# A linear-attention recurrence with a feed-forward layer: a fixed instruction order and a software pipeline

## The chip, the core and the metric

The kernel runs on one core of a Trainium2 chip. Five engines work side by side, each with a queue of instructions of its own: TensorE (PE; its loads of stationary weights are listed as PEld), VectorE (DVE), ScalarE (ACT), GpSimd (POOL) and SyncE (SP), which issues most DMAs. They wait for one another through semaphores. The metric is device time in microseconds (us), and lower is better.

## What is computed

For each of 4 x 8 = 32 heads there is a state matrix of 40 x 40 that is carried through 768 time steps. The result y is then laid out as 3072 tokens of 320 features and goes through a feed-forward layer with squared ReLU.

```
for t in range(768):                       # all 32 heads, head size D = 40
    y[t]  = r[t] @ state
    Sa    = state @ a[t]
    state = state * w[t] - outer(Sa, b[t]) + outer(v[t], k[t])
x   = y as 3072 x 320
out = (relu(x @ w_in) ** 2) @ w_out        # 320 -> 2048 -> 320
```

## The kernel before

Time is cut into 6 chunks of 128 steps (loop variable c). Heads stand in pairs, two of 40 in 128 partitions (the halves 0 to 63 and 64 to 127, index s). A batch has 8 heads, that is 4 pairs; a quad is 2 pairs (4 heads), so a chunk has 4 batches and 8 quads (q), and the kernel 24 batches and 48 quads.

Work falls into three kinds.

- Preparation of a batch (`prep`): six loads of 160 KB (W, K, V, R, A, B; one row per time step and head, 160 bytes each); the logarithm of W on ACT (lnW, line 129); its running sum by a float32 matmul with a triangle (cs, line 132); two exponentials (GI and Gp, lines 135 and 136); casts of R, V, A and products of K, B with GI on POOL (lines 137 to 141); twenty transposes on PE (line 146) into t1 (R and V), t2 (Gp and K) and t3 (A); copies of these to SBUF on ACT (RVT line 155, GT line 160, KT line 161), and AT on DVE (line 164).
- A quad: `stage1` forms two 128 x 128 products per head (ec, lines 185 and 189; contraction over half of the partitions), which DVE masks into EVC (lines 193 and 194). `stage2` takes the carried state: z = state times R (line 207), copied by ACT into UZ (line 209); mx from AT and UZ (line 214, half of the rows) and from EVC (line 219, all rows), masked by DVE into MX (line 224); then uy collects an identity times UZ (IDb, line 227), K times EVC (line 232) and B times MX (line 237), the last two with half of the columns each. DVE scales uy into the next state UZ (line 241) and the output YS (line 244), and ut (line 250) turns the state for the next chunk's z, copied into UBD by two ACT instructions (line 253).
- The feed-forward layer of a chunk: `gather` brings YS into token order with eight DMAs (X<-YS, line 275); `ffn_in` is called 16 times (j), each with three hp matmuls (line 283), a relu on ACT (hs, line 287) and a square on DVE or POOL in turn (Gt, line 289); `ffn_out` is called 4 times, each with 16 op matmuls (line 295), an ACT copy (line 298) and a store.

The main loop writes, per quad, stage1 of the next quad, stage2 of this one, two or three `ffn_in` (or `ffn_out`) of the chunk before, and after each odd quad a preparation of the next chunk. All four batches of chunk 0 are prepared ahead of the loop, the weights are loaded behind that on POOL's queue. The last chunk's feed-forward layer stands alone behind the loop. A scheduler then reorders each engine's instructions; in PSUM five banks are shared by everything of the recurrence and of the preparation (pool `ps`), three by hp and op (pool `pf`).

Of the kernel before, what the change touches and what calls it, by code (L numbers as in the profile page):

```python
# [15 lines left out]
def kernel(  # L16
# [49 lines left out]
    MU4 = gl.tile([128, 2, 2, 128], BF16, name="MU4")  # L66
# [19 lines left out]
    for key in ("R", "A", "G", "V", "K", "B"):  # L86
        for i in range(2):
            heads = NHH if key in "RAG" else NH
            t_ = gl.tile([128, heads, 64], BF16, name=f"{key}p{i}")
            nc.any.memset(t_[:, :, D:64], 0.0)  # L90
            pads[key, i] = t_
    UZs = [gl.tile([128, NP, VC], BF16, name=f"UZ{i}") for i in range(2)]
# [4 lines left out]
    LOADS = ("W", "K", "V", "R", "A", "B")

    def load(c):
        got = {}  # L100
        for bb in range(NB):
            for key in LOADS:
                t_ = natp.tile([128, NHH, D], FP32, name=f"N{key}", tag=f"N{key}", bufs=5)
                nc.sync.dma_start(
                    out=t_[:],
                    in_=nat_srcs[key][bb, :, c * L:(c + 1) * L, :].rearrange("h t e -> t h e"))
                got[key, bb] = t_
        return got

    class Chunk:  # L110
        pass

    def chunk_tiles(c):
        ch = Chunk()
        ch.c = c
        ch.RV, ch.KT, ch.AT, ch.GT = [], [], [], []
        ch.EVC = {}
        ch.YS = chp.tile([128, NP, L], BF16, name="YS", tag="YS")
        ch.p = {key: pads[key, c % 2] for key in "KBV"}
        return ch  # L120

    def prep(ch, bb, nat):

        h0 = bb * NHH
        hs = slice(h0, h0 + NHH)
        P = ch.p
        Rp, Ap, Gp = (pads[key, bb % 2] for key in "RAG")
        lnW = ffp.tile([128, NHH * D], FP32, name="lnW", tag="lnW", bufs=2)
        nc.scalar.activation(out=lnW[:], in_=nat["W", bb][:].rearrange("p h e -> p (h e)"),  # L129
                             func=ACTF.Ln)  # L130
        cs = ps.tile([128, NHH, D], FP32, name="cs", tag="ps")
        nc.tensor.matmul(out=cs[:].rearrange("p h e -> p (h e)"), lhsT=UTI[:], rhs=lnW[:],  # L132
                         start=True, stop=True)
# [233 lines left out]
```

## Time and profile before

| | us |
|---|---|
| median of 3 runs (lowest, highest) | 369.28 (368.61, 370.23) |
| the profiled execution | 370.21 |
| its span, first to last instruction | 368.5 |
| PE busy | 308.7 |
| ACT busy | 187.0 |
| DVE busy | 171.3 |
| POOL busy | 142.0 |

The mean granted clock of PE is 0.943 of full speed. A matmul's duration in the trace includes the time through the array, and successive matmuls overlap; what one costs is read from the start of the next. Times in the rows are counted from the start of the span.

### The profile page before, as it was taken

What the parts mean: (1) busy time and instruction counts of PE and PEld (TensorE: products, weight loads), DVE (VectorE), ACT (ScalarE), POOL (GpSimd) and SP (SyncE); (2) the same over time, 40 slices, a digit from 0 to 9 for tenths busy, and PEclk for the clock granted to TensorE, in tenths of its full rate; (3) what the DMA queues carried; (4) which work ended last, traced back from release to release, by engine and by line L of the source; (5) the groups of instructions that cost most, each with busy time, mean ns of one, the idle gap of its engine ahead of it and who ended that gap; (6) DMA issues with size and microseconds to landing.
All of it is one profiled execution on the core that took longest, in us unless ns stands there. A gap on an engine that the chain in (4) does not pass through costs nothing. (4 is left out here: it accounts for less than half of the span.)

```text
span 368.5 us, 7042 instructions
## 1 busy us (share of the span) xinstructions
PE 308.7 (84%) x2600; PEld 163.2 (44%) x2600; DVE 171.3 (46%) x461; ACT 187.0 (51%) x392; POOL 142.0 (39%) x253
## 2 busy tenths in 40 slices
PE   2512676778799999999998999998999999999896
PEld 1302443444344555444554344554445545445454
DVE  3000346443745641854543854545673446873140
ACT  4521442444177555767355686346776536441371
POOL 4523533333165533465233465123554203430170
PEclk9999956655899999999999999999999999999999
DMA  9999999993852973972562551131000111001202
GB/s 151 178 153 175 180 185 178 179 163 69 125 105 39 154 133 87 165 124 41 109 125 62 83 91 25 49 64 46 0 3 0 37 45 29 3 2 50 58 2 72
DMA packets 163859, 32.58 MB, mean 88 GB/s; under 512 B 158384, under 2 KB 163504, under 8 KB 163824
## 3 DMA queue, kind: packets, MB, share of 16 engines
q1 hardware_dynamic: 161376, 29.50, 45.0%
q0 software_dynamic: 2448, 2.62, 4.6%
q8 instruction: 20, 0.33, 0.4%
q14 instruction: 15, 0.12, 0.1%
HBM read 28.84 MB, written 3.93 MB: 89 GB/s over the span
## 5 line engine op out<-in xcount | busy, mean ns | idle before, releaser
L283 PE MATMUL hp<-X,WIN 120*128 120x512 bf16 (+1 forms) x288 | 80.3, 384 | 1.9 <-DMA X<-YS 0.9
L287 ACT ACTIVATE hs<-hp 128x512 bf16<-128x512 f32 x96 | 55.2, 600 | 39.3 <-PE hp L283 30.5
L289 POOL TENSOR_TENSOR Gt<-hs 128x512 bf16<-128x512 bf16 x48 | 50.2, 1048 | 64.3 <-ACT hs L287 55.8
L253 ACT ACTIVATE UBD<-ut 40x256 bf16<-40x256 f32 x80 | 30.2, 377 | 47.4 <-PE ut L250 46.6
L193 DVE TENSOR_TENSOR EVC<-ec,MU 128x256 bf16<-128x256 f32 x96 | 40.0, 416 | 30.4 <-PE ec L189 29.2
L164 DVE TENSOR_TENSOR AT<-t,GT 128x512 bf16<-128x512 bf16 x24 | 10.1, 423 | 91.3 <-ACT GT L160 72.9
L224 DVE TENSOR_TENSOR MX<-mx,MX 128x336 bf16<-128x336 f32 x96 | 43.9, 499 | 13.2 <-PE mx L219 13.0
L179 POOL COPY EVC<-Vp 128x160 bf16<-128x160 bf16 x48 | 15.7, 330 | 87.1 <-PE uy L232 80.2
L194 DVE TENSOR_TENSOR EVC<-ec,MU 128x256 bf16<-128x256 f32 x96 | 39.8, 414 | 0.0
L295 PEld LDWEIGHTS <-Gt 128*128 128x128 bf16 x384 | 32.2, 98 | 15.0
L237 PE MATMUL uy<-MX,Bp 128*64 128x168 bf16 x192 | 29.3, 264 | 8.7 <-DVE MX L224 8.2
L289 DVE TENSOR_TENSOR Gt<-hs 128x512 bf16<-128x512 bf16 x48 | 27.3, 570 | 19.9 <-ACT hs L287 19.5
L283 PEld LDWEIGHTS <-WIN 120*128 120x128 bf16 (+1 forms) x288 | 23.0, 98 | 23.5 <-issue 2.7
L132 PE MATMUL cs<-lnW,UTI 128*128 128x320 f32 x48 | 24.2, 593 | 8.9 <-ACT lnW L129 8.9
L155 ACT ACTIVATE RVT<-t 128x1024 bf16<-128x1024 bf16 x24 | 24.7, 1029 | 12.9 <-PE t L146 12.8
L237 PEld LDWEIGHTS <-Bp 128*64 128x64 bf16 x192 | 13.1, 112 | 36.3 <-issue 36.0
L219 PE MATMUL mx<-EVC 128*128 128x168 bf16 x192 | 24.9, 252 | 1.4 <-DVE EVC L194 0.9
L140 POOL TENSOR_TENSOR Kp<-NK,GI 128x320 bf16<-128x320 f32 x24 | 20.6, 859 | 11.5 <-ACT GI L135 11.5
L137 POOL CAST Rp<-NR 128x320 bf16<-128x320 f32 x24 | 10.8, 449 | 30.8 <-DMA NR<-in_r_dram 16.5
L244 DVE TENSOR_TENSOR YS<-uy,GT 128x256 bf16<-128x256 f32 x48 | 20.0, 417 | 5.2 <-PE uy L237 5.1
L146 PE MATMUL t<-IDb,Rp 128*128 128x128 bf16 x96 | 11.2, 250 | 13.2 <-POOL Rp L137 13.2
L141 POOL TENSOR_TENSOR Bp<-NB,GI 128x320 bf16<-128x320 f32 x24 | 20.6, 859 | 2.5 <-DMA NB<-in_b_dram 2.5
(110 smaller groups left out, 448.1 us busy)
## 6 DMA issues: line engine op xcount, KB each, us to landing
NW<-in_w_dram SPq DMA_DIRECT2D x24, 160.0 KB
NK<-in_k_dram SPq DMA_DIRECT2D x24, 160.0 KB
NV<-in_v_dram SPq DMA_DIRECT2D x24, 160.0 KB
NR<-in_r_dram SPq DMA_DIRECT2D x24, 160.0 KB
NA<-in_a_dram SPq DMA_DIRECT2D x24, 160.0 KB
NB<-in_b_dram SPq DMA_DIRECT2D x24, 160.0 KB
out_dram<-osb SPq DMA_DIRECT2D x24, 160.0 KB
X<-YS SPq DMA_DIRECT2D x48, 40.0 KB
```

The lines of the kernel that those rows point to most:

```text
L132: nc.tensor.matmul(out=cs[:].rearrange("p h e -> p (h e)"), lhsT=UTI[:], rhs=lnW[:], start=True, stop=True)
L155: nc.scalar.activation(out=RV[:], in_=t1[:], func=ACTF.Copy)
L193: nc.vector.tensor_tensor(out=dst[:, :, 0:L], in0=ec[s][:, 0], in1=MU4[:, 0], op=ALU.mult)
L194: nc.vector.tensor_tensor(out=dst[:, :, L + D:], in0=ec[s][:, 1], in1=MU4[:, 1], op=ALU.mult)
L219: nc.tensor.matmul(out=mx[s][:, i, :], lhsT=EVC[:, i, s, 0:L], rhs=EVC[:, i, s, L:], start=(c == 0), stop=True, skip_group_check=True)
L224: nc.vector.tensor_tensor(out=MX[:, s], in0=mx[s][:], in1=MX2[:], op=ALU.mult)
L237: nc.tensor.matmul(out=uy[half(s), i, :], lhsT=ch.p["B"][:, 4 * q + 2 * i + s, :], rhs=MX[:, s, i, :], start=False, stop=True, skip_group_ ...
L253: nc.scalar.activation(out=UBD[64 * s:64 * s + D, p2, :], in_=ut[64 * s:64 * s + D, :, :], func=ACTF.Copy)
L283: nc.tensor.matmul(out=hp[:], lhsT=WIN[g][0:rows[g], j * 128:(j + 1) * 128], rhs=ch.X[g][0:rows[g]].rearrange("p a b -> p (a b)"), start=( ...
L287: nc.scalar.activation(out=hs[:], in_=hp[:], func=ACTF.Relu)
L289: eng.tensor_tensor(out=ch.Gt[:, j].rearrange("p a b -> p (a b)"), in0=hs[:], in1=hs[:], op=ALU.mult)
L295: nc.tensor.matmul(out=op_[:], lhsT=ch.Gt[:, j, bb, :], rhs=WOUT[:, j, :], start=(j == 0), stop=(j == NJ - 1))
```

## The change

The order of each engine's instructions is taken as the code writes it (`manual_schedule`). The code is cut into parts, and a step per quad writes them: ec of the next quad, z and IDb, a filler, ut of the quad before, mx, a filler, parts of a preparation, K, B, a filler, further parts. A filler is one `ffn_in` or half an `ffn_out`; it starts three steps behind the end of its chunk. A table (`when`) says which step prepares which batch; chunk 0 starts after one batch. The loads are issued batch by batch, six ahead; the weights after step 5, the gather in two parts (after quads 5 and 7), the last one from three queues.

In PSUM ec, mx and uy get banks of their own with one buffer each (five banks), hp and op two, and t1, t2, t3, cs and ut share one (`pp`; in the first five batches the preparation uses those of hp). z is formed in uy's bank and stays there as a part of the sum, so that IDb carries only the state's columns. One mask instruction per half covers both products of ec; UZ is scaled in two halves; UBD is copied in one instruction. A square is issued one piece later than its relu. UZ is set to zero at the start by POOL.

```diff
-    ps = ctx.enter_context(tc.tile_pool(name="ps", bufs=5, space=PSUM))
-    pf = ctx.enter_context(tc.tile_pool(name="pf", bufs=3, space=PSUM))
+    ps = ctx.enter_context(tc.tile_pool(name="ps", bufs=1, space=PSUM))
+    ctx.enter_context(tc.manual_schedule())
...
+    def load(m):
+
+        c, bb = divmod(m, NB)
+        for key in ("W", "K", "B", "R", "V", "A"):
+            t_ = natp.tile([128, NHH, D], FP32, name=f"N{key}", tag=f"N{key}")
+            nc.sync.dma_start(
+                out=t_[:],
+                in_=nat_srcs[key][bb, :, c * L:(c + 1) * L, :].rearrange("h t e -> t h e"))
+            nat[key, m] = t_
+
+    AHEAD = 6
+    for m in range(AHEAD):
+        load(m)
...
+        t_ = gl.tile([128, NP, UWP], BF16, name=f"UZ{i}")
+        nc.gpsimd.memset(t_[:], 0.0)
...
+    def where_pp(m):
+        return {"tag": "ff", "bufs": 2} if m < 5 else {"tag": "pp"}
...
+        if m + AHEAD < NBC:
+            load(m + AHEAD)
...
+    def prep_rv(m):
+        o = bt[m]
+        o.RV = chp.tile([128, 2, PB, L], BF16, name="RVT", tag="RVT", bufs=4)
+        t1 = ps.tile([128, 2, PB, L], BF16, name="t1", **where_pp(m))
...
+        ec = [ps.tile([128, 2, 2, L], FP32, name=f"ec{s}", tag=f"ec{s}") for s in range(2)]
...
-            nc.vector.tensor_tensor(out=dst[:, :, 0:L], in0=ec[s][:, 0], in1=MU4[:, 0], op=ALU.mult)
-            nc.vector.tensor_tensor(out=dst[:, :, L + D:], in0=ec[s][:, 1], in1=MU4[:, 1],
-                                    op=ALU.mult)
...
+            nc.vector.tensor_tensor(out=spread(EVC[:, :, s, 0:L], L + XO[s]), in0=ec[s][:],
+                                    in1=MU4[:].rearrange("p (i u) x -> p i u x", u=2), op=ALU.mult)
+
+    def st_z(st):
+
+        c, o, j0, p2 = where(st)
+        UZ = UZs[c % 2]
+        uy = uys[st] = ps.tile([128, 2, UW], FP32, name="uy", tag="uy")
         if c > 0:
-            z = ps.tile([128, 2, L], FP32, name="z", tag="ps")
             for i in range(2):
-                nc.tensor.matmul(out=z[:, i, :], lhsT=UBD[:, 2 * q + i, :],
-                                 rhs=ch.RV[bb][:, 0, j0 + i, :], start=True, stop=True)
-            nc.scalar.activation(out=UZ[:, p2, D:VC], in_=z[:], func=ACTF.Copy)
-        mx = [ps.tile([128, 2, VC], FP32, name=f"mx{s}", tag="ps") for s in range(2)]
+                nc.tensor.matmul(out=uy[:, i, D:D + L], lhsT=UBD[:, p2.start + i, :],
+                                 rhs=o.RV[:, 0, j0 + i, :], start=(i == 0), stop=False,
+                                 skip_group_check=True)
+            nc.scalar.activation(out=UZ[:, p2, D:D + L], in_=uy[:, :, D:D + L], func=ACTF.Copy)
+        nc.tensor.matmul(out=spread(uy[:, :, 0:D], VC), lhsT=IDb[:],
+                         rhs=spread(UZ[:, p2, 0:D], VC), start=(c == 0), stop=False,
+                         skip_group_check=True)
...
+        mx = [ps.tile([128, 2, VC], FP32, name=f"mx{s}", tag=f"mx{s}") for s in range(2)]
...
-            nc.tensor.matmul(out=uy[:].rearrange("p a b -> p (a b)"), lhsT=IDb[:],
-                             rhs=UZ[:, p2, :].rearrange("p a b -> p (a b)"),
-                             start=True, stop=False, skip_group_check=True)
...
+        for s in range(2):
+            for i in range(2):
+                nc.tensor.matmul(out=uy[half(s), i, D * s:D * s + VC],
+                                 lhsT=o.B[:, 2 * (j0 + i) + s, :], rhs=MX[:, s, i, :],
+                                 start=False, stop=True, skip_group_check=True)
...
+            for u in range(2):
+                nc.vector.tensor_tensor(
+                    out=UZs[(c + 1) % 2][half(u), p2, VC * u:VC * u + D],
+                    in0=uy[half(u), :, VC * u:VC * u + D],
+                    in1=gl_[half(u)].to_broadcast([64, 2, D]), op=ALU.mult)
...
+        ut = ps.tile([128, 2, 128], FP32, name="ut", tag="pp")
...
+        nc.scalar.activation(out=UBD[:, p2, :], in_=ut[:], func=ACTF.Copy)
...
+        hp = ps.tile([128, NB * L], FP32, name="hp", tag="ff", bufs=2)
...
+        later.append(lambda: eng.tensor_tensor(out=Gt[:, j].rearrange("p a b -> p (a b)"),
+                                               in0=hs[:], in1=hs[:], op=ALU.mult))
...
+    def ffn_out(c, bb, part):
+        flush()
+        if part == 0:
+            ops[c, bb] = ps.tile([128, DM], FP32, name="op_", tag="ff", bufs=2)
+        op_ = ops[c, bb]
+        for j in range(part * NJ // 2, (part + 1) * NJ // 2):
...
+    def filler(st):
+        if fill and fill[0][0] <= st:
+            fill.pop(0)[1]()
...
+    when = {}
+    for m in range(1, NBC):
+        first = 2 * m - 2 if m < 5 else {5: 8, 6: 10, 7: 11}.get(m, 2 * m - 4)
+        last = first if 5 <= m < 8 else first + 1
+        for st, lot, f in ((first, 0, prep_cast), (first, 1, prep_decay), (first, 2, prep_rv),
+                           (last, 1, prep_gk), (last, 2, prep_a)):
+            when.setdefault((st, lot), []).append((f, m))
+    def prepare(st, lot):
+        for f, m in when.pop((st, lot), []):
+            f(m)
+    for f in (prep_cast, prep_decay, prep_rv, prep_gk, prep_a):
+        f(0)
+    st_ec(0)
+    for st in range(NS):
+        c, q = divmod(st, NQ)
+        late = c == 0 and q % 2 == 1
+        prepare(st, 0)
+        if not late and st + 1 < NS:
+            st_ec(st + 1)
+        st_z(st)
+        filler(st)
+        if st > 0:
+            st_u(st - 1)
+        st_mx(st)
+        filler(st)
+        prepare(st, 1)
+        st_k(st)
+        st_b(st)
+        filler(st)
+        prepare(st, 2)
+        if late:
+            st_ec(st + 1)
+        if st == 5:
+            load_weights()
+        if q == 5:
+            gather(c, 0, 3, [nc.sync])
+        if q == 7:
+            gather(c, 3, 4, [nc.sync] if c + 1 < NCH else [nc.sync, nc.scalar, nc.gpsimd])
+            fill += [(st + 3, lambda c=c, j=j: ffn_in(c, j)) for j in range(NJ)]
+            fill += [(st + 3, lambda c=c, b_=b_, p_=p_: ffn_out(c, b_, p_))
+                     for b_ in range(NB) for p_ in range(2)]
+    flush()
+    while fill:
+        fill.pop(0)[1]()
```

On PE, at the end of a quad of chunk 1 (K and B into uy, op of the feed-forward layer), there stood before:

```order
L295 LDWEIGHTS Gt_1054
L295 MATMUL op__1659<-WOUT_124,Gt_1054 128x320
L237 LDWEIGHTS Bp1_118
L237 MATMUL uy_1537<-MX_1534,Bp1_118 64x168
L295 LDWEIGHTS Gt_1054
L295 MATMUL op__1659<-WOUT_124,Gt_1054 128x320
L295 LDWEIGHTS Gt_1054
L295 MATMUL op__1659<-WOUT_124,Gt_1054 128x320
L237 LDWEIGHTS Bp1_118
L237 MATMUL uy_1537<-MX_1534,Bp1_118 64x168
L237 LDWEIGHTS Bp1_118
L237 MATMUL uy_1537<-MX_1534,Bp1_118 64x168
```

On PE, at the same place of a quad of chunk 1, there stands now:

```order
L260 MATMUL uy_1598<-EVC_1482,Kp3_191 64x168
L260 LDWEIGHTS Kp3_191
L260 MATMUL uy_1598<-EVC_1482,Kp3_191 64x168
L270 LDWEIGHTS Bp3_199
L270 MATMUL uy_1598<-MX_1626,Bp3_199 64x168
L270 LDWEIGHTS Bp3_199
L270 MATMUL uy_1598<-MX_1626,Bp3_199 64x168
L270 LDWEIGHTS Bp3_199
L270 MATMUL uy_1598<-MX_1626,Bp3_199 64x168
L270 LDWEIGHTS Bp3_199
L270 MATMUL uy_1598<-MX_1626,Bp3_199 64x168
L353 LDWEIGHTS Gt_1045
```

The four B matmuls (line 237, now 270) were split by op matmuls and stood apart from K; now they follow K without a break, and the feed-forward work comes behind them.

On SP, around the gather of chunk 0 (X), there stood before, behind 66 loads:

```order
L104 DMA NW_501<-in_w_dram 128x8x40
L104 DMA NK_503<-in_k_dram 128x8x40
L104 DMA NV_505<-in_v_dram 128x8x40
L104 DMA NR_507<-in_r_dram 128x8x40
L104 DMA NA_509<-in_a_dram 128x8x40
L104 DMA NB_511<-in_b_dram 128x8x40
L275 DMA X0_974<-YS_176 40x4x128 x3
L275 DMA X1_975<-YS_176 40x4x128 x3
L275 DMA X2_976<-YS_176 40x4x128 x2
```

On SP, at the gather of chunk 0, there stands now, behind 60 loads:

```order
L320 DMA X0_706<-YS_345 40x3x128 x3
L320 DMA X1_707<-YS_345 40x3x128 x3
L320 DMA X2_708<-YS_345 40x3x128 x2
L63 DMA NW_761<-in_w_dram 128x8x40
L63 DMA NK_763<-in_k_dram 128x8x40
L63 DMA NB_765<-in_b_dram 128x8x40
L63 DMA NR_767<-in_r_dram 128x8x40
L63 DMA NV_769<-in_v_dram 128x8x40
L63 DMA NA_771<-in_a_dram 128x8x40
L320 DMA X0_706<-YS_345 40x128 x3
L320 DMA X1_707<-YS_345 40x128 x3
L320 DMA X2_708<-YS_345 40x128 x2
```

The gather stood behind twelve batches of loads; its first part now stands behind ten, its second behind eleven.

## Rows read from the trace of the kernel before

**Rows 1.** Stretches: length, PE, PEld, DVE, ACT, POOL busy, clock, DMA, GB/s.

```profile
0.00:80.00 80.00, 42.45 (x308) 25.77 (x310) 23.87 (x71) 30.35 (x62) 30.68 (x74) 0.83 1.08 171
42.00:105.00 63.00, 46.35 (x387) 26.92 (x385) 31.27 (x89) 25.54 (x56) 21.19 (x48) 0.67 0.89 142
105.00:335.00 230.00, 218.22 (x1946) 110.06 (x1944) 128.05 (x344) 133.13 (x283) 94.77 (x154) 1.00 0.34 65
```

**Rows 2.** Timeline of PE, one quad: start, length, instructions, idle time and what ended it.

```profile
218.09 0.26 PE L237 MATMUL uy<-MX,Bp 128*64 128x168 bf16 x1
218.28 0.61 PE L283 MATMUL hp<-X,WIN 120*128 120x512 bf16 x2
218.82 0.33 PE L237 MATMUL uy<-MX,Bp 128*64 128x168 bf16 x3
219.08 0.82 PE L283 MATMUL hp<-X,WIN 120*128 120x512 bf16 x3
219.84 0.29 PE L250 MATMUL ut<-IDS,UZ 128*40 128x128 bf16 x4
220.06 0.29 PE L185 MATMUL ec<-AT,KT 64*128 64x128 bf16 x4
...
220.39 0.29 PE L207 MATMUL z<-RVT,UBD 128*128 128x128 bf16 x2
220.51 0.81 PE L283 MATMUL hp<-X,WIN 120*128 120x512 bf16 x3
221.65 0.32 PE L214 MATMUL mx<-UZ,AT 64*128 64x168 bf16 x4 [0.32 <-ACT UZ L209]
221.90 0.46 PE L219 MATMUL mx<-EVC 128*128 128x168 bf16 x4
222.20 0.31 PE L227 MATMUL uy<-UZ,IDb 128*128 128x336 bf16 x1
222.44 0.34 PE L232 MATMUL uy<-EVC,Kp 128*64 128x168 bf16 x4
222.71 0.82 PE L283 MATMUL hp<-X,WIN 120*128 120x512 bf16 x3
```

**Rows 3.** The chain that ended last, its end: start, length, what.

```profile
344.60 2.12 DMA X<-YS
...
347.25 0.61 ACT hs L287
...
347.90 8.63 PE hp L283 x39
...
363.05 2.19 PE op__5046 L295 x16
```

**Rows 4.** Timeline of PE, the preparation of a batch.

```profile
212.00 0.81 PE L132 MATMUL cs<-lnW,UTI 128*128 128x320 f32 x2
212.65 0.39 PE L146 MATMUL t<-IDb,Rp 128*128 128x128 bf16 x4
212.87 0.39 PE L146 MATMUL t<-IDb,Vp 128*128 128x128 bf16 x4
...
214.43 0.40 PE L146 MATMUL t<-IDb,Kp 128*128 128x128 bf16 x4 [0.30 <-POOL Kp L140]
```

**Rows 5.** Timeline of PE, two quads of chunk 0 apart, and the first hp.

```profile
60.00 0.36 PE L185 MATMUL ec<-AT,KT 64*128 64x128 bf16 x4
...
71.65 0.40 PE L185 MATMUL ec<-AT,KT 64*128 64x128 bf16 x4
...
99.95 1.34 PE L283 MATMUL hp<-X,WIN 120*128 120x512 bf16 x3
```

**Rows 6.** Groups by line: busy time, mean ns of one, idle time before.

```profile
L155 ACT ACTIVATE RVT<-t 128x1024 bf16<-128x1024 bf16 x24 | 24.7, 1029 | 12.9 <-PE t L146 12.8
```

**Rows 7.** Timeline of all engines, the first AT.

```profile
12.22 0.42 DVE L164 TENSOR_TENSOR AT<-t,GT 128x512 bf16<-128x512 bf16 x1 [7.66 <-ACT GT L160]
```

**Rows 8.** Timeline of SP, the issue of chunk 0's gather.

```profile
84.33 6.89 SPq L275 DMA_DIRECT2D X<-YS  x8
```

More of the change, by code (lines that the diff above doesn't have):

```diff
@@ L85 @@
-    pads = {}
[L86 to L92, printed above, removed]
-    UBD = gl.tile([128, NP, 128], BF16, name="UBD")
-    nc.any.memset(UBD[:], 0.0)
-    nat_srcs = {"W": w, "K": k, "V": v, "R": r, "A": a, "B": b}
@@ L97 @@
[L97 to L110, printed above, removed]
-        pass
[L113 to L120, printed above, removed]
@@ L143, in transposes @@
-        def transposes(dst, pad, h):
-            for j in range(PB):
-                src = pad[:, h + 2 * j:h + 2 * j + 2, :].rearrange("p a b -> p (a b)")
-                nc.tensor.transpose(out=dst[:, j, :], in_=src, identity=IDb[:])
-        RV = chp.tile([128, 2, PB, L], BF16, name="RVT", tag="RVT", bufs=8)
-        KT = chp.tile([128, PB, L], BF16, name="KT", tag="KT", bufs=8)
-        AT = chp.tile([128, PB, L], BF16, name="AT", tag="AT", bufs=8)
-        GT = chp.tile([128, PB, L + 2], BF16, name="GT", tag="GT", bufs=8)
@@ L230, in stage2 @@
         for i in range(2):
             for s in range(2):
[L232 to L234 removed]
+                nc.tensor.matmul(out=uy[half(s), i, D * s:D * s + VC],
+                                 lhsT=o.K[:, 2 * (j0 + i) + s, :], rhs=EVC[:, i, s, L:],
+                                 start=False, stop=False, skip_group_check=True)
@@ L257 @@
-    WIN = []
+                nc.tensor.matmul(out=ut[half(s), i, :],
+                                 lhsT=UZn[:, p2.start + i, VC * s:VC * s + 64],
+                                 rhs=IDb[:], start=True, stop=True)
+        nc.scalar.activation(out=UBD[:, p2, :], in_=ut[:], func=ACTF.Copy)
+    YSs, Xs, Gts, WIN = {}, {}, {}, []
     rows = [3 * D, 3 * D, 2 * D]
@@ L333 @@
-    for j in range(NJ):
-        ffn_in(prev, j)
-    for bb in range(NB):
-        ffn_out(prev, bb)
+        Gt = Gts[c]
+        later.append(lambda: eng.tensor_tensor(out=Gt[:, j].rearrange("p a b -> p (a b)"),
+                                               in0=hs[:], in1=hs[:], op=ALU.mult))
+    ops = {}
+    def ffn_out(c, bb, part):
[4 more added lines that the diff above has]
+        for j in range(part * NJ // 2, (part + 1) * NJ // 2):
+            nc.tensor.matmul(out=op_[:], lhsT=Gts[c][:, j, bb, :], rhs=WOUT[:, j, :],
+                             start=(j == 0), stop=(j == NJ - 1))
+        if part == 1:
+            osb = ffp.tile([128, DM], FP32, name="osb", tag="osb")
+            nc.scalar.activation(out=osb[:], in_=op_[:], func=ACTF.Copy)
+            tok = bb * T + c * L
+            nc.sync.dma_start(out=out[tok:tok + L, :], in_=osb[:])
```

275 lines of the change are left out of this document (132 added, 143 removed).

## The prediction

> **What bounds the kernel now.** I read three views in this order: busy time by stretch, the order of matmuls on TensorE (PE) within one quad, and the sync queue (SP). The stretches [rows 1] show two regimes. From 105 to 335 us PE is busy 218.2 of 230.0 us at the full granted clock: the end is set by how much PE must do and by what its hand-overs cost. From 42 to 105 us it is busy 46.4 of 63 us and the clock is granted at 0.67 on average, between its levels of 1.2 and 2.4 GHz: here PE waits in each quad for VectorE (DVE). The DMA engines move 171 GB/s over the first 80 us, nothing of which is spare: 13.7 MB. The weights' share of it is 2 x 2048 x 320 numbers of two bytes, 2.62 MB.
>
> Within a quad of the busy stretch [rows 2] the starts tell more than the durations, since matmuls are pipelined. Three hp take 0.22 us each, but from the third to a ut, which uses 40 of the array's columns, it takes 0.10 us more (219.08 to 219.84). The same 0.10 us stands at every change between full-array, half-row (ec, mx from AT) and half-column (K, B, ut) matmuls; z to hp, both full, shows none (0.12 us for two z). A quad of before changes eleven times.
>
> **The stretch with feed-forward work, steps 10 to 47 (a step is a quad).** By starts in [rows 2] one quad of before costs PE: B 0.19 and 0.26 (split around hp), ut 0.22, ec 0.33, z 0.12, mx 0.25 and 0.30, the IDb matmul 0.24, K 0.27, together 2.18, and four entries from hp at 0.10: 2.58 us. Afterwards B follows K with nothing between (K 0.27 - 0.10 = 0.17; B 0.07 + 0.26 = 0.33), and IDb moves 160 columns for 336 (0.14 less its change, halved: 0.07) and stands behind z without a change. That is 0.33 + 0.12 + 0.07 + 0.22 + 0.25 + 0.30 + 0.17 + 0.33 = 1.79, with three entries 2.09 us. The saving is 0.49 us per quad. All other terms stay: an hp 0.22 (8.63 us for 39), an op 0.136 (2.19 for 16) [rows 3], a preparation 0.65 for cs and five times 0.22 for its transposes, 1.75 us [rows 4].
>
> Steps 10 to 47 hold 38 quads, 18 preparations (batches 6 to 23) and 114 pieces: 80 of ffn_in (three hp, 0.66 us) and 34 halves of ffn_out (eight op, 1.09 us). PE's sum: 38 x 2.09 = 79.4, less 7 x 0.22 where the last chunk has no ut, = 77.9; 52.8; 37.0; 18 x 1.75 = 31.5. Together 199.2 us.
>
> Stalls come on top. Before, from the first hp at 99.95 [rows 5] to the last chunk's X at 346.7 [rows 3], 246.8 us pass. The same prices give 38 x 2.58 - 8 x 0.32 = 95.4 for quads, 5 x 19.3 = 96.4 for five chunks of feed-forward and 16 x 1.75 = 28.0 for the preparations that the code leaves for it: 219.8. So 27 us, 0.71 per quad, were waits: mx for ScalarE's (ACT) copy of z (0.32 at 221.65 [rows 2]), the transposes of Kp for GpSimd (POOL) (0.30 at 214.43 [rows 4]). Both places now have a filler and other parts between. But the order is fixed, so nothing else can step in, and ec, mx, uy have one buffer each, while cs, t1, t2, t3 and ut share one bank: each of the six uses in two steps waits until ACT has read the one before, behind ACT's relus. The longest such read is 1.03 us (RVT [rows 6]). The bound from below is 0, from above 1.1 us per step (that read once per step, fully exposed). I take 0.5, nearer to the 0.71 of before less the waits with cover: 34 steps with preparations, 17 us. Batches 6 and 7 go through all parts in one step; there Kp's transposes wait for Exp and multiply as before, and K and B of the quad stand behind: 1.5 us each (0 to 3), 3 us.
>
> DVE: one mask of 512 elements replaces two of 256, UZ's scaling becomes two instructions: less than a tenth of a microsecond either way per quad, hidden while DVE is below PE (128.1 of 230 us [rows 1]). The single UBD copy takes work from ACT; I cost both at nothing. If ACT or DVE were full, that is the first rival.
>
> **The start.** In before all four batches are prepared before the first quad, and weights move between the loads. Afterwards quad 0 needs batch 0 alone. Before's first AT is ready at 12.6 us [rows 7]. Two new memsets of 3712 elements on POOL stand ahead of its first casts and delay this; I put quad 0 at 13 to 20 us. Two quads with a preparation took 11.65 us at the low clock (60.00 to 71.65 [rows 5]); the new pairs have the same chain (masks, MX, YS). Five pairs bring step 10 to 72 to 79 us.
>
> Step 10 holds the first hp, and that needs X. Here **a new wait** comes. On SP the gather's second half stands behind batch 10's loads, and each DMA waits for the one eight places ahead to land. So X needs 11 batches x 0.983 MB = 10.81, the weights' 2.62 (POOL's queue, after step 5) and 0.25 for the first half: 13.68 MB. At 171 GB/s [rows 1] that is 80 us; the last gather's issue (6.89 us for eight [rows 8], so 0.86) and landing (2.12 us [rows 3]) make it 83, and I take 84 (80 to 88). PE's queue is in order, so mx, K and B of step 10 and all behind wait with the hp. Whether step 10 is reached at 65 or 80 us is then worth nothing; putting the weights later gains little, since their bytes are still ahead of X. The wait probably lowers the clock again: 2 us (0 to 4).
>
> **The tail.** Six pieces of chunk 4, all ffn_out halves, are left after step 47: 6 x 1.09 = 6.5 us, which cover the last gather (landing 2.12 us, three queues). Then sixteen ffn_in: the ff pool has two buffers instead of three, so a relu (0.61 us with its hand-over in [rows 3], about 0.7) sets the pace rather than 0.66: 11.5 us. Eight halves 8.7. Together 26.7 us. From the last matmul to the end of the span 368.5 - 365.2 = 3.3 us stay [rows 3].
>
> **The sum.** 84 + 2 + 199.2 + 17 + 3 + 26.7 + 3.3 = 335 us of span. The profiled execution took 370.21 us for a span of 368.5, and the median of the runs is 0.9 below it; so 335 + 1.7 - 0.9 = 336 us. Against before that is 16 us from the earlier first hp, some 25 from quads and waits behind it, and 8 back in the tail, of which 6.5 are work moved there.
>
> **The rivals.** First, ACT through the shared bank sets the pace: stalls of 1.1 us in each of 34 steps instead of 0.5, 20 us more, 356 us. For it speaks that six uses of one bank per two steps each take a read by ACT; against it that ACT was busy 133.1 of 230 us [rows 1] and that op steps leave it idle.
>
> Second, X comes early: the queue moves faster than in before, or the transfers of loads and weights overlap better, and PE reaches the first hp at its own pace near 68 us. That gives 320 us. Against it stand the 171 GB/s, at a DMA share above 1 [rows 1].
>
> Third, on the slow side: the clock. Where before had a wait of about a microsecond in each quad, 42 to 105 us, the granted clock was 0.67 [rows 1]; where PE was busy 95% it was 1.00. With one buffer for each of five banks, waits in every step could bring that state to steps 10 to 47. Some 165 of the 199 us are streaming, which takes twice as long at 1.2 GHz, so from about a fifth of the stretch at the low level (34 us) the change loses; at a third of it the time is 390 us. Against it: the sum above leaves PE about 90% busy.
> On this the Trainium skill, TensorE: Matmul & The Clock Gate, section "A second HAM failure mode: psum-queue depth-cycling", speaks against the change: cycling through PSUM banks makes PE idle briefly between groups often enough that its clock swings between the two levels. By that rule the third rival would be the likeliest and the time near its 390; the trace of before, with its own cycling of five banks at clock 1.00 from 105 to 335 us, does not bear it out.
>
> **How the numbers follow.** Forecast 0.60 (336 us, by its own bounds 318 to 348); first rival 0.18 (356); second 0.13 (320); third 0.05 (390); 0.04 for faster stretches than all of these (stalls near 0, below 318). The range of 310 to 358 leaves out the third rival and the ends of the others. The low end is X at 80, stalls of 3 us and no loss in relus: 80 + 199.2 + 3 + 25 + 3.3 + 0.8 = 311; the high end is the first rival with 2 us more for X. Faster by over 0.5% (about what a measurement of this kernel can tell from no change): 0.60 + 0.18 + 0.13 + 0.04 less 0.02 for stalls that eat it all, 0.93; the same 0.02; slower 0.05.
>
> **What would show it.** The first hp in the new trace at 80 to 88 us, with PE idle before it for 5 us or more and an X DMA as what ended it; no more than three entries per quad, B 0.17 us behind K; two steps with ffn_in pieces 10.5 to 11 us apart, with ffn_out 12.5 to 13; hp in the tail 0.7 us per piece. The prediction is wrong if the first hp starts by 75 us (then the second rival), if PE idles over 1 us per step on ACT behind cs, t or ut (the first), or if the granted clock is below 1.00 in the stretch after the first hp (the third).

## The result

The changed kernel takes 359.34 us (median of 4, 358.58 to 360.8) against 369.75 us before in the same comparison: ratio 0.973, 95% interval 0.968 to 0.977. It is faster, by 10 us and not by the 33 forecast; 336 us and the range up to 358 were both too low.

The same three stretches as in [rows 1], of the kernel after (length, PE, PEld, DVE, ACT, POOL busy, clock, DMA share, GB/s):

```profile
0.00:80.00 80.00, 46.80 (x409) 29.07 (x409) 44.85 (x109) 25.25 (x50) 34.05 (x71) 0.75 1.06 165
42.00:105.00 63.00, 35.14 (x249) 19.38 (x248) 20.45 (x46) 15.59 (x32) 13.90 (x32) 0.57 0.87 140
105.00:335.00 230.00, 202.22 (x2019) 120.04 (x2019) 125.35 (x293) 126.79 (x265) 104.21 (x193) 1.00 0.35 69
```

The clock is at its upper level from 105 us on, as before. But PE is busy for 202.2 of 230 us there instead of 218.2: some 12% of the stretch is idle. What PE waited for is in the next view, five rows of PE's waits over the whole span (waiting line, released by: us in total, times, longest):

```profile
PE uy L231 <- ACT UZ L230: 26.4, 40, 0.9
PE hp L335 <- DMA X<-YS: 16.3, 3, 13.8
PE ec L207 <- DVE AT L186: 5.9, 7, 1.1
PE t L162 <- ACT RVT L170: 3.3, 3, 1.1
PE t L162 <- ACT Gp L152: 2.7, 3, 0.9
```

The second row is the wait for X that was forecast. The first is in no term of the sum: L231 is the IDb matmul, and L230 is ACT's copy of z. Every one of the 40 quads that have a z pays it. In the timeline of PE over two steps (start, length, instructions, idle time and its end; to be held against [rows 2]) it looks like this:

```profile
165.50 0.28 PE L207 MATMUL ec<-AT,KT 64*128 64x128 bf16 x4
...
165.82 0.28 PE L227 MATMUL uy<-RVT,UBD 128*128 128x128 bf16 x2
167.05 0.23 PE L231 MATMUL uy<-UZ,IDb 128*128 128x160 bf16 x1 [0.94 <-ACT UZ L230]
167.12 0.81 PE L335 MATMUL hp<-X,WIN 120*128 120x512 bf16 x3
...
169.84 0.34 PE L260 MATMUL uy<-EVC,Kp 128*64 128x168 bf16 x4
170.01 0.31 PE L270 MATMUL uy<-MX,Bp 128*64 128x168 bf16 x4
170.26 0.82 PE L335 MATMUL hp<-X,WIN 120*128 120x512 bf16 x3
...
171.85 0.29 PE L227 MATMUL uy<-RVT,UBD 128*128 128x128 bf16 x2
172.61 0.23 PE L231 MATMUL uy<-UZ,IDb 128*128 128x160 bf16 x1 [0.47 <-ACT UZ L230]
...
177.15 0.28 PE L207 MATMUL ec<-AT,KT 64*128 64x128 bf16 x4
```

From z to IDb 1.23 us pass in one step and 0.76 in the next, where the sum had 0.12. The longer one is the step in which ACT reads RVT (1.02 us) ahead of z. Two steps take 11.65 us (165.50 to 177.15), not 10.5 to 11. The rest of the quad is as priced: B 0.17 us behind K, three entries from full-array matmuls.

IDb and the copy touch no common column: IDb writes columns 0 to 40 and 168 to 208 of each half of uy, ACT reads 40 to 168. The program holds a semaphore between them all the same. Two things are shared, the bank of uy and the tile UZ in SBUF, of which IDb reads columns 0 to 40 and 168 to 208 and the copy writes those between; which of the two makes the wait is tried below (z twice). On the bank the Trainium skill, PSUM — Partial Sum Buffer, section "PSUM bank collisions raise a hardware error", says that two engines have to be kept apart by bank (within each 32 partitions) and not by address, since disjoint columns collide too. The trace agrees as far as it can: the wait stands in all 40 quads. By that page it can't be left out, and no run here leaves it out; the order and the bank can be chosen.

PE's start of the feed-forward work and the steps behind it, to be held against the last row of [rows 5]:

```profile
70.76 0.29 PE L231 MATMUL uy<-UZ,IDb 128*128 128x160 bf16 x1 [0.47 <-ACT UZ L230]
84.82 0.58 PE L335 MATMUL hp<-X,WIN 120*128 120x512 bf16 x1 [13.78 <-DMA X<-YS]
87.07 0.59 PE L335 MATMUL hp<-X,WIN 120*128 120x512 bf16 x1 [1.66 <-DMA X<-YS]
88.55 0.59 PE L335 MATMUL hp<-X,WIN 80*128 80x512 bf16 x1 [0.89 <-DMA X<-YS]
...
99.97 0.29 PE L207 MATMUL ec<-AT,KT 64*128 64x128 bf16 x4 [0.58 <-DVE AT L186]
...
110.62 0.29 PE L207 MATMUL ec<-AT,KT 64*128 64x128 bf16 x4
```

The first hp starts at 84.82 us, forecast 84. X comes in three parts and is whole only at 88.55, and steps 10 and 11 then last until 110.62.

### The profile page after: what moved, and what is told of

Same layout as the page of the kernel before. It is cut to its first block, busy times and chain, and to the rows that moved or that the text cites. A ratio compares the mean times of both kernels' runs of the same rounds, so it can differ in the third digit from the quotient of the medians.

```text
span 356.9 us, 7113 instructions
## 1 busy us (share of the span) xinstructions
PE 281.4 (79%) x2608; PEld 165.9 (46%) x2608; DVE 178.3 (50%) x421; ACT 168.4 (47%) x345; POOL 151.4 (42%) x280
## 4 chain that ended last, share of the span: by engine, by line
PE 61%; ACT 16%; DVE 7%; issue 7%; SPq 5%; POOL 1%; DMA 1%; ACTq 0%; DVEq 0%; POOLq 0%
PE hp L335 15%; PE t L162 6%; PE mx L248 6%; ACT hs L339 4%; ACT UZ L230 4%; PE cs L148 4%; SPq L320 3%; PE uy L231 3%; PE uy L260 3%; PE mx L243 3%; DVE EVC L217 3%; ACT RVT L170 3%; PE ut L294 3%; PE uy L270 2%; SPq L63 2%
## 5 line engine op out<-in xcount | busy, mean ns | idle before, releaser
L335 PE MATMUL hp<-X,WIN 120*128 120x512 bf16 (+1 forms) x288 | 80.3, 391 | 16.9 <-DMA X<-YS 16.3
L217 DVE TENSOR_TENSOR EVC<-ec,MU 128x512 bf16<-128x512 f32 x96 | 61.7, 684 | 22.4 <-PE ec L211 17.4
L231 PE MATMUL uy<-UZ,IDb 128*128 128x160 bf16 x48 | 11.8, 246 | 26.8 <-ACT UZ L230 26.4
L170 ACT ACTIVATE RVT<-t 128x1024 bf16<-128x1024 bf16 x24 | 24.5, 1020 | 13.7 <-PE t L162 13.7
L342 DVE TENSOR_TENSOR Gt<-hs 128x512 bf16<-128x512 bf16 x48 | 20.9, 435 | 17.6 <-ACT hs L339 17.4
L207 PE MATMUL ec<-AT,KT 64*128 64x128 bf16 x192 | 15.5, 229 | 11.8 <-DVE AT L186 5.9
L215 POOL COPY EVC<-Vp 128x80 bf16<-128x80 bf16 x96 | 24.0, 279 | 0.0
L297 ACT ACTIVATE UBD<-ut 128x256 bf16<-128x256 f32 x40 | 15.2, 379 | 18.3 <-PE ut L294 18.3
L178 ACT ACTIVATE GT<-t 128x512 bf16<-128x512 bf16 x24 | 14.3, 598 | 18.8 <-PE t L162 18.7
L230 ACT ACTIVATE UZ<-uy 128x256 bf16<-128x256 f32 x40 | 15.4, 385 | 11.3 <-PE uy L227 10.6
L280 DVE TENSOR_TENSOR UZ<-uy,GT 64x80 bf16<-64x80 f32 x80 | 18.7, 234 | 0.5
L270 PE MATMUL uy<-MX,Bp 128*64 128x168 bf16 x192 | 17.6, 249 | 0.2
```

What stands on the lines that cost most here:

```text
L170: nc.scalar.activation(out=o.RV[:], in_=t1[:], func=ACTF.Copy)
L217: nc.vector.tensor_tensor(out=spread(EVC[:, :, s, 0:L], L + XO[s]), in0=ec[s][:], in1=MU4[:].rearrange("p (i u) x -> p i u x", u=2), op=AL ...
L230: nc.scalar.activation(out=UZ[:, p2, D:D + L], in_=uy[:, :, D:D + L], func=ACTF.Copy)
L270: nc.tensor.matmul(out=uy[half(s), i, D * s:D * s + VC], lhsT=o.B[:, 2 * (j0 + i) + s, :], rhs=MX[:, s, i, :], start=False, stop=True, ski ...
L335: nc.tensor.matmul(out=hp[:], lhsT=WIN[g][0:rows[g], j * 128:(j + 1) * 128], rhs=Xs[c][g][0:rows[g]].rearrange("p a b -> p (a b)"), start= ...
L342: later.append(lambda: eng.tensor_tensor(out=Gt[:, j].rearrange("p a b -> p (a b)"), in0=hs[:], in1=hs[:], op=ALU.mult))
```

## Experiments: the wait of the IDb matmul

**IDb ahead of z.** Theory W: the IDb matmul's wait for ACT in uy's bank is what is missing. Rival A is the first rival of the prediction: ACT and the shared bank set the pace.

```
+        nc.tensor.matmul(out=spread(uy[:, :, 0:D], VC), lhsT=IDb[:],
+                         rhs=spread(UZ[:, p2, 0:D], VC), start=True, stop=False,
...
         if c > 0:
...
-                                 rhs=o.RV[:, 0, j0 + i, :], start=(i == 0), stop=False,
+                                 rhs=o.RV[:, 0, j0 + i, :], start=False, stop=False,
...
             nc.scalar.activation(out=UZ[:, p2, D:D + L], in_=uy[:, :, D:D + L], func=ACTF.Copy)
-        nc.tensor.matmul(out=spread(uy[:, :, 0:D], VC), lhsT=IDb[:],
-                         rhs=spread(UZ[:, p2, 0:D], VC), start=(c == 0), stop=False,
...
```

> Edit: the IDb matmul is issued ahead of the two z matmuls instead of behind them; it now clears the uy bank, z adds to it. Nothing else moves. Theory W (the IDb matmul waits for ScalarE's copy of z in the same bank: 26.4 us in 40 quads of the changed kernel, 22.2 of them in 33 quads between 120 and 320 us): the wait goes, the filler follows z at once and covers the copy, two steps with ffn_in come down from 11.65 to 10.3 to 10.7 us, the time to 333 to 340 us. Rival A (ScalarE and the bank that cs, t1 to t3 and ut share set the pace): the same waits come back at ut, mx or the transposes, two steps stay at 11.3 us or more, the time at 354 to 359 us.

329.73 us (329.56 to 330.06), ratio to before 0.890 (0.885 to 0.894): 30 us less than the changed kernel, by one matmul that stands three rows higher. PE of this kernel, the start of one step and of the step two before it, then the stretch from 120 to 280 us, and below it the same stretch of the kernel after:

```profile
115.67 0.29 PE L207 MATMUL ec<-AT,KT 64*128 64x128 bf16 x4
...
125.61 0.28 PE L207 MATMUL ec<-AT,KT 64*128 64x128 bf16 x4
...
125.94 0.24 PE L225 MATMUL uy<-UZ,IDb 128*128 128x160 bf16 x1
126.02 0.28 PE L230 MATMUL uy<-RVT,UBD 128*128 128x128 bf16 x2
126.13 0.81 PE L335 MATMUL hp<-X,WIN 120*128 120x512 bf16 x3
```

```profile
120.00:280.00 160.00, 158.88 (x1679) 97.90 (x1678) 105.38 (x250) 103.87 (x222) 85.78 (x164) 1.00 0.43 83
```

```profile
120.00:280.00 160.00, 141.03 (x1453) 84.46 (x1452) 93.31 (x223) 92.59 (x196) 77.51 (x146) 1.00 0.41 79
```

PE has no idle time left (158.9 of 160 us). The wait doesn't come back elsewhere: of mx for the copy there are two waits of 0.4 us together. Two steps take 9.94 us (115.67 to 125.61), less than the 10.3 that was expected at least.

**IDb behind mx.** The same matmul, in the other direction: from behind z to behind the mx matmuls.

```
-        nc.tensor.matmul(out=spread(uy[:, :, 0:D], VC), lhsT=IDb[:],
...
+        nc.tensor.matmul(out=spread(uys[st][:, :, 0:D], VC), lhsT=IDb[:],
...
         MX = mxs[st] = qdp.tile([128, 2, 2, VC], BF16, name="MX", tag="MX")
```

> Edit: the IDb matmul is issued behind the mx matmuls from EVC, between the first filler and the second, instead of right behind z. Theory W: as with the IDb matmul ahead of z, 333 to 340 us, since filler and mx lie between the copy of z and its reader in the bank; it may be some us better, since z is not delayed by 0.07 us. Rival A: 354 to 359 us.

331.16 us (328.59 to 332.07), ratio 0.892 (0.887 to 0.897), not to be told from IDb ahead of z. Both places do it, so it is the place directly behind z that costs, not the matmul.

**z twice.** The order of the changed kernel stays, IDb right behind z; only the bank that ACT reads is another.

```
+            z = ps.tile([128, 2, L], FP32, name="z", tag="pp")
+            for i in range(2):
+                nc.tensor.matmul(out=z[:, i, :], lhsT=UBD[:, p2.start + i, :],
+                                 rhs=o.RV[:, 0, j0 + i, :], start=True, stop=True)
-            nc.scalar.activation(out=UZ[:, p2, D:D + L], in_=uy[:, :, D:D + L], func=ACTF.Copy)
+            nc.scalar.activation(out=UZ[:, p2, D:D + L], in_=z[:], func=ACTF.Copy)
```

> Edit to the changed kernel: z is made twice, once in uy as before, and right behind it into the bank of cs, t1 to t3 and ut, from which ScalarE copies it; the IDb matmul stands behind both as in the changed kernel. Theory W in its sharper form (it is the copy's reading in the same bank, not the place behind z, that the IDb matmul waits for): the wait goes although the order stays; two matmuls more per quad cost 0.12 us each quad, some 5 us in 40: 333 to 342 us. If the place behind z is what costs, 357 to 366 us. If uses of the shared bank wait for ScalarE (Rival A), one more use per step shows there: 345 us or more, with the waits at cs, t or ut.

347.96 us (347.73 to 349.03), ratio 0.939 (0.934 to 0.943). PE's waits, two rows:

```profile
PE hp L339 <- DMA X<-YS: 18.4, 3, 15.9
PE z L232 <- ACT RVT L170: 10.2, 16, 0.7
```

Among all waits of PE none of the IDb matmul for ACT is left, though the copy still writes UZ, and IDb still reads it, as before. So the bank makes the wait, and not UZ. In its place stands one that both theories had a part in: the second z waits for ACT's read of RVT out of the shared bank, 10.2 us in 16 steps. With 40 x 0.12 us for the matmuls, 329.7 + 4.8 + 10.2 = 344.7, 3 us less than measured. By starts the second z costs more than its recorded waits: it comes 0.94 us behind the first in a step that waits (162.95 to 163.89) and 0.32 in one that doesn't (168.81 to 169.13), where z alone takes 0.12. That is enough for the rest. The time, 348 us, lies where Rival A had it, and part of it is Rival A's kind of wait: uses of the shared bank do wait when one more is put in; with the six per two steps that the changed kernel has, they don't once the IDb matmul is out of the way.

**The scheduler's order.** The code of the changed kernel without the fixed order.

```
-    ctx.enter_context(tc.manual_schedule())
```

> Edit to the changed kernel: the fixed order is dropped, the scheduler orders each engine from the same code; on TensorE it puts an hp piece between z and the IDb matmul where one is at hand. Theory W: the wait of the IDb matmul mostly goes, the time is 328 to 342 us, so the fixed order as written costs more than it brings. Rival (the fixed order is where the changed kernel's gain comes from): 360 us or more.

337.62 us median, with the four runs from 326.0 to 341.65, all below the changed kernel's; they spread too far to say by how much. The order of the times is that of the mean granted clock, from 0.968 at 326.0 us to 0.889 at 341.65. IDb now stands behind other work, an hp or op piece or ut, and in the execution profiled (335.97 us) its wait shrinks to this row:

```profile
PE uy L231 <- ACT UZ L230: 1.1, 5, 0.5
```

PE's wait for X, 16.3 us in the changed kernel, is gone from the list too: quads go on in its place, and the first hp starts at 106.69 us. So this kernel differs by more than the one wait. The fixed order as written was not where the gain came from; it nailed one matmul to a place where the scheduler slipped other work between, 0.66 us for an hp piece.

**More work for ACT.** On top of IDb ahead of z, one unused copy in each of 29 steps, ahead of the copy of ut.

```
+        if st > 10:
+            idle = ffp.tile([128, 512], BF16, name="idle", tag="idle")
+            nc.scalar.activation(out=idle[:], in_=MU4[:].rearrange("p a b -> p (a b)"), func=ACTF.Copy)
         nc.scalar.activation(out=UBD[:, p2, :], in_=ut[:], func=ACTF.Copy)
```

> On top of the IDb matmul ahead of z (329.7 us): from step 11 on ScalarE makes one more copy of 512 elements (some 0.5 to 0.6 us each, about 19 us in all) in every step that has a ut, ahead of its copy of ut out of the shared bank; the result is not used. If ScalarE and the shared bank set the pace (Rival A), all or most of it shows: 341 to 350 us. If they have room once the IDb matmul doesn't wait: 329 to 333 us.

332.15 us (330.99 to 333.27), ratio 0.895 (0.892 to 0.899), against 0.890 (0.885 to 0.894) without. The group of the added copies and the stretch from 120 to 280 us:

```profile
L299 ACT ACTIVATE idle<-MU 128x512 bf16<-128x512 bf16 x29 | 18.2, 628 | 0.0
```

```profile
120.00:280.00 160.00, 159.47 (x1659) 95.90 (x1658) 102.79 (x244) 116.85 (x246) 83.47 (x160) 1.00 0.45 84
```

Of 18.2 us 2.4 show by the medians, 3.8 by the two executions profiled (327.8 and 331.6 us of span). ACT isn't the bound, and Rival A falls for this kernel.

## Experiments: X, the clock and steps 10 and 11

**X through ACT's queue.**

```
-            gather(c, 0, 3, [nc.sync])
+            gather(c, 0, 3, [nc.scalar] if c == 0 else [nc.sync])
```

and the same for the second half.

> Edit: the sixteen small DMAs that gather chunk 0's X are issued by ScalarE's queue instead of the sync queue, where they stood behind the loads of batches 9 and 10. Theory X (the order of the sync queue makes the first hp wait until 84.8 us, and the wait costs clock behind it): the first hp starts at 66 to 72 us, with no wait for X above 1 us; the time falls by 14 to 22 us, to 337 to 345 us. Rival (the bytes ahead of X set it, or sixteen issues on ScalarE hold up the copies of steps 5 to 8): the first hp starts at 78 us or later, the time is 350 to 359 us.

361.32 us (361.18 to 362.22), ratio 0.975 (0.971 to 0.979): nothing gained, worse than either theory. ACT in this kernel (ACTq is the issuing of DMAs):

```profile
38.56 1.43 ACTq L320 DMA_DIRECT2D X<-YS  x1
...
40.03 22.42 ACTq L320 DMA_DIRECT2D X<-YS  x7
62.49 0.47 ACT L140 ACTIVATE lnW<-NW 128x320 f32<-128x320 f32 x1 [22.91 <-DMA X<-YS]
```

Seven issues held ACT for 22.4 us, and batch 4's preparation behind them; the first hp starts at 91.70 us, later than the 84.82 of the changed kernel. In the trace the DMAs of SP and ACT take their semaphores from the same eight, so that one of them waits on its semaphore for an earlier one, whichever engine issued it: ACT issues at 42.15 and 52.14 us, each time 0.02 us after the landing (42.13, 52.12) of a load that SP had issued at 37.06 and 37.71. This was not tried by itself. The Trainium skill, DMA: Bandwidth & Descriptors, section "Issuing engines are not separate DMA queues", says that DMAs of all issuers run on the same 16 engines and that another issuer saves only its issuing time; here it cost more than that, since the issuing engine itself was held.

**Both edits.**

> Edit: both, the IDb matmul ahead of z and chunk 0's gather on ScalarE's queue. If the two waits are separate costs, the gains add: with 18 to 24 us for the first and 14 to 22 us for the second the time is 313 to 327 us. If the second wait only moves what ScalarE holds up anyway (Rival A), the sum is less than the parts by 8 us or more: above 330 us.

328.68 us (326.46 to 330.41), ratio 0.886 (0.881 to 0.892), between the two ranges. What X by ACT gives alone, nothing, it gives here too; the sum of parts was expected from a part that isn't there. PE no longer waits for X, and one wait of 17.7 us for ACT's lnW stands in its place.

**Loads behind the gather.** On top of IDb ahead of z, the loads of batches 9 and 10 are issued behind chunk 0's gather.

```
+    HELD = (3, 4)
...
-        if m + AHEAD < NBC:
+        if m + AHEAD < NBC and m not in HELD:
             load(m + AHEAD)
...
             gather(c, 3, 4, [nc.sync] if c + 1 < NCH else [nc.sync, nc.scalar, nc.gpsimd])
+            if c == 0:
+                for m in HELD:
+                    load(m + AHEAD)
```

> On top of the IDb matmul ahead of z (329.7 us): the loads of batches 9 and 10 are issued behind chunk 0's gather on the sync queue, instead of ahead of its halves. Theory X (the first hp waits for X because X stands behind these loads, on the sync queue or, when ScalarE issues it, through the wait of each DMA for an earlier one): the first hp starts at 66 to 73 us instead of 85.4, and 10 to 20 us go: 310 to 320 us. Rival (X comes at 80 us or later by the bytes in flight, or what is held back comes late for steps 14 and 16): 322 to 332 us.

320.19 us (317.78 to 322.22), ratio 0.863 (0.857 to 0.870). PE at the first hp, the stretch from 58 to 80 us, and the issue of X on SP:

```profile
74.76 0.59 PE L336 MATMUL hp<-X,WIN 120*128 120x512 bf16 x1 [6.37 <-DMA X<-YS]
77.66 0.58 PE L336 MATMUL hp<-X,WIN 120*128 120x512 bf16 x1 [2.32 <-DMA X<-YS]
79.12 0.58 PE L336 MATMUL hp<-X,WIN 80*128 80x512 bf16 x1 [0.88 <-DMA X<-YS]
```

```profile
58.00:80.00 22.00, 9.70 (x75) 5.24 (x75) 5.54 (x13) 3.85 (x8) 2.69 (x8) 0.50 0.49 87
```

```profile
64.47 13.44 SPq L321 DMA_DIRECT2D X<-YS  x16
```

X is whole 10.0 us earlier than with IDb ahead of z alone (79.12 against 89.15 there), and the time falls by 9.5 us by the medians, by 11.7 between the executions profiled (327.8 and 316.1 us of span). X's arrival thus counts about one for one. The first hp still starts 2 us behind the 73 expected at the latest, and the last part of X lands 4.4 us behind that, now with the DMA engines half idle (share 0.49): sixteen issues one after the other take 13.4 us of SP's time.

**Unused matmuls ahead of the first hp,** on top of IDb ahead of z, to keep PE's clock up while X comes: 36, and 92.

```
+        if c == 0 and j == 0:
+            for _ in range(36):
+                nc.tensor.matmul(out=hp[:], lhsT=IDb[:], rhs=MU4[:].rearrange("p a b -> p (a b)"),
+                                 start=True, stop=True)
```

> On top of the IDb matmul ahead of z (329.7 us): 36 matmuls of 512 columns, whose result is not used, stand ahead of the first hp of chunk 0, so that PE works while X comes. Steps 10 and 11 took from 89.1 us, when X was complete, to 110.7 us, at a granted clock near 0.5 to 0.6. Theory C (the low clock behind the wait makes these two steps long): they shrink by 5 to 10 us, the time is 320 to 325 us. Rival (the waits of two whole preparations in one step each make them long, the clock little): 328 to 333 us.

> As the run with 36 unused matmuls ahead of the first hp, which ended at 78.1 us, 8 us before X came, so that the clock fell again (granted 0.50 from 90 to 105 us): here 92 of them, which at the full clock end at about 90 us, when X is complete. Theory C (the low clock makes steps 10 and 11 long): the first hp runs at 89 to 91 us at a granted clock of 1.00, step 10 and 11 end at 102 to 106 us instead of 110.7, the time is 322 to 326 us against 329.7 without. Rival (their waits make them long): ends at 109 us or later, 328 to 333 us.

36 of them: 329.99 us (328.26 to 331.1), ratio 0.888 (0.883 to 0.893). They ended 8 us before X came, so this run says nothing of the clock. 92 of them: 327.2 us (325.76 to 330.4), ratio 0.884 (0.878 to 0.890), between the two theories and not to be told from 0.890 (0.885 to 0.894) without them. Stretches with 92: the unused matmuls, step 10, the first part of step 11, its rest:

```profile
68.00:89.00 21.00, 21.00 (x92) 9.20 (x91) 0.42 (x1) 0.10 (x1) 0.00 (x0) 0.93 0.60 99
89.00:98.50 9.50, 6.07 (x54) 3.19 (x54) 2.49 (x7) 5.30 (x10) 4.25 (x8) 0.99 1.16 166
98.50:106.00 7.50, 6.49 (x35) 3.01 (x34) 2.54 (x5) 2.62 (x6) 1.89 (x3) 0.56 0.59 76
106.00:111.00 5.00, 3.82 (x43) 2.21 (x45) 2.41 (x7) 3.45 (x6) 3.60 (x8) 1.00 0.67 116
```

Step 10 runs at full clock now, but PE is busy for 6.07 of 9.5 us in it, and then the clock falls again: step 11 ends at 109.67 instead of 110.72, with X's last part 1.1 us later (90.24 against 89.15). Of the 5 to 10 us of Theory C, that the low clock behind the wait makes these steps long, about 2 are there; most of it falls, and the waits in the steps come first. What a clock kept up through step 11 would give, no run shows.

**X earlier and 42 unused matmuls.**

> The IDb matmul ahead of z, the loads of batches 9 and 10 behind chunk 0's gather (320.2 us with these two; X complete at 79.1 us there), and 42 unused matmuls ahead of the first hp, which at the full clock end at about 80 us. Theory C: another 3 to 7 us go, 313 to 317 us. Rival: 318 to 323 us.

317.6 us (317.14 to 317.82), ratio 0.857 (0.855 to 0.860), against 0.863 (0.857 to 0.870) without: between what the two theories gave. The two traces have the same span, 316.1 us, and step 11 ends at 98.95 with the unused matmuls and at 98.96 without, so no gain is shown.

**Preparations spread, X earlier still.** The loads of batches 7 and 8 behind the gather too, batch 6 prepared in step 9, batch 7 in steps 10 and 11.

```
-    HELD = (3, 4)
+    HELD = (1, 2, 3, 4)
-        first = 2 * m - 2 if m < 5 else {5: 8, 6: 10, 7: 11}.get(m, 2 * m - 4)
-        last = first if 5 <= m < 8 else first + 1
+        first = 2 * m - 2 if m < 5 else {5: 8, 6: 9}.get(m, 2 * m - 4)
+        last = first if 5 <= m < 7 else first + 1
```

> On top of the IDb matmul ahead of z and the loads of batches 9 and 10 behind chunk 0's gather (320.2 us; X complete at 79.1 us, steps 10 and 11 from there to 98.96): the loads of batches 7 and 8 stand behind the gather too, batch 6 is prepared in step 9 instead of 10, and batch 7 in steps 10 and 11 instead of 11 alone. Theory (X waits on the sync queue for loads whose transfers share the DMA engines with the weights; the waits for Gp, Kp and RVT of 1 to 3 us in each of steps 10 and 11 come from a whole preparation in one step): X is complete by 66 to 72 us, TensorE reaches the first hp at 68 to 72 us, the two steps end 12 us or less behind it instead of 20; together 300 to 310 us. Rival (the weights, 2.62 MB, or the held loads come late): hp at 76 us or later, or waits for lnW of batches 7 to 9, 314 to 324 us.

The median of four runs is 311.77 us. Two of them took 307.79 and 309.72 us, within the 300 to 310 expected, with a ratio of 0.834 (0.829 to 0.839), the fastest of all kernels here; the other two took 313.81 and 314.2, above it. The trace is that of the run with 314.2. PE at the first hp and behind step 11:

```profile
74.01 1.48 PE L336 MATMUL hp<-X,WIN 120*128 120x512 bf16 x3
...
84.29 0.29 PE L208 MATMUL ec<-AT,KT 64*128 64x128 bf16 x4
```

The first hp starts without a wait at 74.01 us, which is when PE gets there with more preparation in step 9, and steps 10 and 11 end at 84.29: 10.3 us instead of the 21.6 (89.15 to 110.72) with IDb ahead of z alone. Part of that has moved: step 9, with all of batch 6's preparation in it, takes 10.1 us (63.05 to 73.15), where it takes 3.8 (65.23 to 69.02) with IDb ahead of z alone. What is left over went to chunk 1, whose gather now stands behind the held loads. PE there:

```profile
123.36 0.59 PE L336 MATMUL hp<-X,WIN 120*128 120x512 bf16 x1 [5.73 <-DMA X<-YS]
125.66 0.59 PE L336 MATMUL hp<-X,WIN 120*128 120x512 bf16 x1 [1.72 <-DMA X<-YS]
127.10 0.58 PE L336 MATMUL hp<-X,WIN 80*128 80x512 bf16 x1 [0.85 <-DMA X<-YS]
```

8.3 us of the gain are given back in the same form as the wait that was taken away.

## Why the prediction was wrong

The forecast was 335 us of span, the profiled execution has 356.9. The difference by the sum's own terms, with the kernel that has IDb ahead of z in the last column (its starts come from the same views):

| Stretch | forecast | after | IDb ahead |
|---|---|---|---|
| first hp | 84 | 84.8 | 85.4 |
| from there to the end of step 11 | 17.6 | 25.8 | 25.3 |
| steps 12 to 47, to the first op of the tail | 203.6 | 215.1 | 186.0 |
| tail and end | 30.0 | 31.2 | 31.1 |

(17.6 is two quads of 2.09, six pieces of 0.66, two preparations of 1.75, the 3 us for batches 6 and 7, 2 us of clock and two stalls of 0.5; 203.6 is what is left of 199.2 + 17 + 3 + 2.) The excess is 0.8 + 8.2 + 11.5 + 1.2 = 21.7 us. The starts behind the table that are not shown above, first of the kernel after, then of the one with IDb ahead:

```profile
325.70 2.34 PE L353 MATMUL op__4751<-WOUT,Gt 128*128 128x320 bf16 x16
```

```profile
85.43 0.58 PE L335 MATMUL hp<-X,WIN 120*128 120x512 bf16 x1 [14.83 <-DMA X<-YS]
...
110.72 0.28 PE L207 MATMUL ec<-AT,KT 64*128 64x128 bf16 x4
...
296.68 2.34 PE L353 MATMUL op__4751<-WOUT,Gt 128*128 128x320 bf16 x16
```

**The step that failed** is the one on the IDb matmul: "0.07, stands behind z without a change". Its streaming time was right (0.08 between starts in the kernel with IDb ahead). That z's new bank puts a reader on another engine between the two matmuls was not asked. The rows ahead of the prediction had the price: in [rows 2] z starts at 220.39, and mx, which needs ACT's copy of it, at 221.65 after 0.32 us of idling, with hp in between. Whatever waits for this copy and stands right behind z is stopped for about a microsecond. Here that is 24.5 us of recorded idle time in steps 12 to 47, and 29.1 us by starts (215.1 - 186.0): each wait costs 0.1 to 0.2 us more than its recorded idle time, as the last section shows.

**The stalls** of 17 us, 0.5 per step, were taken for the shared bank and ACT. There are none: with IDb ahead of z, 186.0 us pass where the prices alone gave 187.6. The false term hid 16 us of the missing one; without it the forecast would have been off by less in its terms and more in its sum. The prices themselves held within a per cent: 0.66 per piece, 1.09 per half and 1.75 per preparation give 9.89 us for two steps where 9.94 were measured. Only B behind K came out lower (0.25 from its start to the next, not 0.33).

**The first rival** (356 us, chance 0.18) named the right engine and nearly the time, for a wrong reason: its place was the bank of cs, t1 to t3 and ut. Its sign, PE idle for over 1 us per step on ACT behind cs, t or ut, did not appear; the wait was behind z. That the measured 359 lies next to its 356 is luck: it comes from the missing wait and steps 10 and 11, less the false stalls. A time that fits a rival doesn't confirm it.

**The first hp** came out at 84.8 as forecast, and X ended the wait. The mechanism was half right. The queue order sets it, but not the bytes alone: with two batches of loads behind the gather X came at 79.1 us with the DMA engines half idle. And X's last part lands 3.7 us behind the first hp's start, which the sum left out.

**Batches 6 and 7 and the clock,** 3 and 2 us in the sum, cost more: the two steps are 8.2 us over, 3.7 of them X's last part, 0.5 the IDb wait of step 11, and 4 these terms. Spread preparations brought the pair down to 10.3 us though PE came to it at a clock of 0.50, while a PE at full clock with the old place of the preparations gained about 2 us. So the 3 us for whole preparations in one step were the mis-sized term. The low clock comes behind such waits (0.56 in the first part of step 11 after a step 10 at 0.99 with PE busy 6.07 of 9.5 us), and the two can't be parted further with these runs.

**The tail** was close: 16 ffn_in pieces took 12.45 us (332.22 to 344.67), 0.78 each instead of 0.72. The third rival, the low clock in steps 10 to 47, did not come but for steps 10 and 11 (0.60 from 84.8 to 105 us): 1.00 from 105 us on, with PE 12% idle. The rule of the Trainium skill named with it, TensorE: Matmul & The Clock Gate, section "A second HAM failure mode: psum-queue depth-cycling", isn't borne out here either, as 36 waits of 0.5 to 0.9 us in that stretch left the clock at its upper level.

With the wait taken out the change brings 329.7 us against the forecast of 336. That is near for two reasons that offset each other: some 16 us of stalls that aren't there, and the 7.7 us by which steps 10 and 11 are over.

## What to carry over

When a result is moved into the bank of another, list who reads that bank and what PE issues next into it: here the matmul behind ACT's read waited for it in every quad, though it wrote other columns. In a fixed order, put work of other banks between the two, or the later matmul first; the scheduler did so here by itself. And where a time fits one of the rivals, look at which line waits before believing it.

## What was not expected of the hardware

Seven DMA issues of 30 KB each held ACT for 22.4 us, two of them until loads that SP had issued were in. One short wait per step costs more than its recorded idle time: 0.47 us of idle goes with 0.65 us between starts (0.76 where 0.11 passes in the kernel with IDb ahead). In the profiled execution of the kernel with the scheduler's order PE was busy for 43.4 of 48 us from 42 to 90 us and its clock was still granted at 0.50, so that a high busy share in a trace doesn't by itself show a high clock. The execution that took 326.0 us, at a mean clock of 0.968, can't have had this stretch (48 us at 0.50 leave 0.93 at most):

```profile
42.00:90.00 48.00, 43.44 (x313) 25.05 (x314) 26.13 (x63) 16.58 (x34) 15.95 (x40) 0.50 0.91 142
```
